# Keys of an attention kernel turned by DMA instead of TensorE, with the written order of work remade

## The chip, the cores and the metric

The kernel runs on one core of a Trainium2 chip. The metric is the time of one execution on the device in microseconds (us). The kernel before the change takes 297.64 us (median of three runs, 297.6 to 297.93). A core has five engines that run side by side and meet through semaphores: TensorE (PE, matmuls; PEld is its weight loading), VectorE (DVE), ScalarE (ACT), GpSimd (POOL) and SyncE (SP, which here only issues transfers). Transfers run on 16 DMA engines that all issuers share.

## The reference

Inputs are q, k, v of shape (4, 8, 768, 64) and two MLP weights, 512 x 2048 and 2048 x 512, all float32. For each batch and head the keys are averaged over 12 blocks of 64; each query takes the three blocks with the best gate score, and its own block:

```python
k_rep = k.reshape(B, H, n_blocks, block, D).mean(axis=3)
gate_scores = np.einsum('bhsd,bhnd->bhsn', q, k_rep)
gate_scores = np.where(causal, gate_scores, -1000000000.0)
top_idx = np.argsort(gate_scores, axis=-1)[..., -top_k:]
# mask: the chosen blocks and the own block, and causal
attn = softmax(where(mask, scale * q @ k.T, -1e9));  x = attn @ v
```

The heads are laid side by side (4, 768, 512) and go through a Fourier mixing layer:

```python
mixed = np.real(np.fft.fft(np.fft.fft(x, axis=1), axis=2))
u = x + mixed
un = (u - mean) / np.sqrt(var + 1e-06)
out = u + np.maximum(un @ w_ch1, 0.0) @ w_ch2
```

## The kernel before

**Tiling.** Work is cut into 16 head pairs P = 0 to 15, four for each of four batches. A pair's q and k come as float32 tiles of 128 positions x (6 position tiles, 2 heads, 64), a load of 192 KB for each head, and v in one load of 384 KB. For both q and k, PE transposes six 128x128 float32 tiles into PSUM (`a_tp`, L292; work items `tk` and `tq`). Of K's transposed tile DVE sums each 64 columns (`a_sums`, `ks`, L297), `a_half` (`kh`) splits these sums by head into the gate's weights, and ACT casts K to float16 into one of three slots `qk_s` (`a_k`, `kc`, L308 or L311). Of q's tile DVE makes a float32 copy (`a_q32`, `qc`, L316), which the gate uses, and GpSimd casts it into the slot (`a_q`, `qs`, through the helper `pcopy`, L225).

**Gate.** `g_mm` (`g`) multiplies q by the block sums in four strips of 32 columns, DVE turns the result (`gt`), takes the eight largest of each row (`gx`), compares (`gl`) and turns back (`gm`). For pairs 0 to 6 (`P < NX`) the mask is added to the scores by extra matmuls (L421). For pairs 7 to 15 it is copied by GpSimd into rows 64 to 95 of the slot (`stage_K`, item `K`), and one matmul of 96 rows makes score and mask together (L414); the key side of those 32 rows holds constant block indicators, loaded once a slot (L719, L733).

**Attention.** Scores of a pair come in six tiles (`s`), ACT takes exp (`e`, L431), GpSimd clears the part above the diagonal (`d`, L437), PE multiplies by v cast to float16 (`vc` on GpSimd, `v` on PE), and DVE divides (`x`). DVE folds the batch's x (`fs`, `fd`, `f`), PE does the two Fourier steps (`y`, L519; `m`, L552), DVE adds x (`u`), ACT centres (`xu`), and the result is transposed (`xt` on PE for batch 0; `un` by DMA, L593, for the others). The MLP is `w` (L629, L631), ReLU `r`, `c` (L656) and `o`, and SP stores (`od`).

**Order.** Nothing is scheduled by the program itself: the string `ORDER` lists all work items by hand, and each engine executes its own instructions in that order, waiting where an operand is missing. SP's transfers stand in one queue in that order too, and so do GpSimd's instructions, the weight loads that it issues included (`W` for three parts of w1, `X` for two halves of w2). PSUM has four tiles of two banks for everything. The first MLP matmul closes a first stretch in which the first batch's attention (and part of the second's) runs alone.

Of the kernel before, what the change touches and what calls it, by code (L numbers as in the profile page):

```python
# [11 lines left out]
FP = mybir.dt.float32  # L12
F16 = mybir.dt.float16
# [15 lines left out]
def _consts_np():  # L29
# [35 lines left out]
    ind = np.zeros((2, 32, S), np.float32)  # L65
    for e in range(2):
        ind[e, 16 * e:16 * e + NB] = nn[:, None] == (s[None, :] // 64)
# [5 lines left out]
                ind=ind.transpose(1, 0, 2).copy().astype(np.float16))  # L73
# [39 lines left out]
Lk:1 Lq:1 Lk:2 Lq:2 tk:0 ks:0 tq:0 Lq:3 Lk:3 kh:0 qc:0 iz:1 tk:1 qs:0 kc:0 g:0 ks:1 iz:0 gt:0 tq:1  # L113
kc:1 gx:0 Lq:4 Lv:0 Lk:4 Lv:1 kh:1 gl:0,0 tk:2 gl:0,1 gm:0 kc:2 qc:1 s:0,3 s:0,2 ks:2 e:0,3 qs:1
tq:2 Lq:5 Lk:5 s:0,5 qc:2 g:1 e:0,5 e:0,2 kh:2 s:0,4 gt:1 qs:2 s:0,0 e:0,4 gx:1 s:0,1 d:0,2 tq:3
gl:1,0 e:0,0 gl:1,1 tk:3 gm:1 e:0,1 d:0,0 qc:3 g:2 d:0,3 kc:3 d:0,5 s:1,5 gt:2 d:0,4 s:1,0 e:1,5
qs:3 ks:3 s:1,4 e:1,0 tq:4 d:0,1 gx:2 vc:0 e:1,4 s:1,3 qc:4 s:1,1 Lv:2 e:1,3 s:1,2 gl:2,0 kh:3
tk:4 gl:2,1 e:1,2 d:1,3 gm:2 g:3 d:1,4 ks:4 d:1,0 v:0 d:1,5 gt:3 vc:1 kc:4 gx:3 e:1,1 s:2,5 Lv:3
Lq:6 LF:0 Lq:7 Lk:6 Lk:7 LT:0 s:2,3 kh:4 gl:3,0 e:2,5 gl:3,1 s:2,4 e:2,3 d:1,1 x:0 tq:5 qs:4 e:2,4
g:4 d:2,3 gm:3 qc:5 s:2,0 d:2,4 s:2,2 d:1,2 e:2,0 gt:4 d:2,5 tk:5 vc:2 gx:4 e:2,2 s:2,1 ks:5 d:2,0  # L120
Lv:4 Lq:8 Lk:8 s:3,1 e:2,1 v:1 gl:4,0 kh:5 gl:4,1 kc:5 d:2,1 gm:4 d:2,2 s:3,2 x:1 e:3,1 vc:3 g:5
e:3,2 Lv:5 Lc:0 d:3,1 s:3,5 gt:5 s:3,0 fs:0,1 e:3,5 s:3,3 d:3,2 gx:5 e:3,0 s:3,4 fs:1,1 tq:6
gl:5,0 e:3,3 fs:0,0 v:2 gl:5,1 fs:1,0 e:3,4 d:3,3 qc:6 d:3,0 s:4,5 x:2 d:3,4 s:4,4 e:4,5 d:3,5
s:4,0 qs:5 v:3 e:4,0 gm:5 fs:2,0 fs:2,1 e:4,4 s:5,5 x:3 s:4,1 e:5,5 s:5,1 e:4,1 fd:2,0 s:4,2 s:5,0
fs:3,1 e:5,1 fs:3,0 s:5,2 fd:2,1 e:5,0 fd:3,1 s:4,3 fd:3,0 e:5,2 tk:6 f:0,1 f:0,2 e:4,3 Lk:9 Lq:9
tk:7 f:0,3 e:4,2 f:0,0 y:0,1 ks:7 pg:0 W:0 kc:6 y:0,0 tr:0,1 d:4,0 kc:7 d:4,4 d:4,5 ks:6 d:5,5
d:4,1 ty:0,1 tr:0,0 s:5,3 d:5,2 s:5,4 d:4,3 kh:6 W:1 ty:0,0 m:0,2 qs:6 e:5,3 u:0,2 m:0,1 vc:4
e:5,4 m:0,0 u:0,1 xu:0,2 d:5,4 tk:8 d:5,1 d:4,2 u:0,0 xu:0,1 d:5,0 xt:0,2 W:2 g:6 un:0,2 xu:0,0
xt:0,1 gt:6 tq:8 un:0,1 kc:8 xt:0,0 qc:8 tq:7 un:0,0 qs:8 v:4 Lq:10 Lk:10 Lv:6 Lq:11 qc:7 bn:0,3
w:0,4 d:5,3 qs:7 bn:0,1 w:0,5 r:0,4 gx:6 ks:8 w:0,6 r:0,5 gl:6,0 kh:7 gl:6,1 x:4 w:0,7 r:0,6 gm:6  # L130
w:0,3 r:0,7 s:6,5 r:0,3 s:6,1 e:6,5 s:6,3 e:6,1 kh:8 s:6,2 fs:4,0 bn:0,4 w:0,2 e:6,2 d:6,1 X:0
e:6,3 g:7 w:0,0 d:6,5 gt:7 r:0,2 d:6,3 vc:6 gx:7 s:6,4 r:0,0 vc:5 s:6,0 e:6,4 tk:9 Li:0 gl:7,0
Lv:7 tq:9 gl:7,1 e:6,0 gm:7 w:0,11 Lq:12 Lv:8 K:7 qc:9 kc:9 g:8 r:0,11 v:5 gt:8 d:6,0 ks:9 w:0,8
qs:9 gx:8 w:0,10 x:5 r:0,8 d:6,4 d:6,2 gl:8,0 s:7,5 s:7,2 r:0,10 kh:9 fs:4,1 w:0,1 bn:0,5 e:7,5
vc:7 e:7,2 tq:10 gl:8,1 Lv:9 r:0,1 X:1 gm:8 s:7,4 qc:10 w:0,15 d:7,2 e:7,4 K:8 bn:0,0 g:9 r:0,15
s:7,0 w:0,9 gt:9 e:7,0 gx:9 vc:8 tq:11 r:0,9 d:7,0 Lv:10 s:7,1 qc:11 d:7,5 tk:10 d:7,4 e:7,1
# [651 lines left out]
```

## Time and profile before

| what | value |
|---|---|
| median of the runs | 297.64 us |
| span of the profiled execution (its own time) | 295.6 us; the rest, 2.0 us, lies outside the span |
| PE transposes of q and k (L292) | 192, busy 27.5 us |
| DVE sums of K (L297) | 16 x 945 ns |
| ACT casts of K (L308 / L311) | 7 x 821 ns / 18 x 792 ns |
| GpSimd selections (L437) / cast copies of q | 96 x 414 ns / 25 x 825 ns |
| DMA transposes of `un` (L593) | 18 of 128x512, landing 2.5 us after issue |
| loads of k and q (192 KB) / v (384 KB) | landing 3.5 and 3.9 / 4.7 us after issue |
| weight loads on GpSimd's queue, 768 KB / 1 MB | landing 8.4 / 10.2 us after issue |

How to read it: a group's mean is the latency of one instruction; matmuls overlap, so a run of them passes faster than their means say. A row of 40 digits is the span in slices of 7.4 us, each digit the busy share in tenths. In a line of the timeline the first two numbers are start and duration, and what stands in brackets is idle time before it and what ended it.

### The profile page before, as it was taken

Reading aid. Unit: us, or ns where it says so; the run is one execution under the profiler, and the core shown is the slowest. Engines: PE = TensorE matmul, PEld = TensorE weight load, DVE = VectorE, ACT = ScalarE, POOL = GpSimd, SP = SyncE. Lnnn points to the kernel's source line nnn. Section 1 sums busy time; section 2 is a strip of 40 time slices with the busy share of each in tenths; the row PEclk is TensorE's granted clock in tenths of the full one; section 3 lists DMA queues with packets and bytes.
Section 4 is the critical chain, followed back from the end, with each engine's and each line's share of the span. In section 5 each row is a group of like instructions: output and inputs, shape, how many; then the busy total and the mean of one; then the engine's idle time right before and its main releaser. Section 6 shows DMA issues by size and latency. Waiting matters only on the chain.

```text
span 295.6 us, 6738 instructions
## 1 busy us (share of the span) xinstructions
PE 286.5 (97%) x2633; PEld 180.2 (61%) x2633; DVE 192.5 (65%) x597; ACT 164.2 (56%) x205; POOL 111.1 (38%) x286
## 2 busy tenths in 40 slices
PE   8899999999999999999999999999999999999995
PEld 4566767765676556656757667446666554555453
DVE  2999999986988638987796577714493282700132
ACT  3698989749578841677788843165524250155000
POOL 2267528528776289064753363220303000110000
PEclk9999999999999999999999999999999999999999
DMA  8999999997999727477000005311000052300023
GB/s 197 268 228 230 262 245 199 195 230 118 226 185 211 168 55 186 118 164 176 3 0 2 0 9 136 38 72 71 2 1 2 32 103 44 142 0 2 0 91 125
DMA packets 93200, 33.53 MB, mean 113 GB/s; under 512 B 85936, under 2 KB 89968, under 8 KB 93168
## 3 DMA queue, kind: packets, MB, share of 16 engines
q1 hardware_dynamic: 87504, 28.47, 40.6%
q0 software_dynamic: 3664, 4.19, 9.1%
q10 hardware_dynamic: 2000, 0.44, 0.7%
q8 instruction: 21, 0.34, 0.5%
q14 instruction: 11, 0.09, 0.1%
HBM read 28.63 MB, written 6.29 MB: 118 GB/s over the span
## 4 chain that ended last, share of the span: by engine, by line
PE 84%; DVE 7%; ACT 6%; DMA 1%; issue 1%; DVEq 0%; ACTq 0%
PE c L656 26%; PE h L629 19%; PE h L631 10%; PE sc L414 7%; PE av L449 6%; ACT pt L431 5%; PE tp L292 5%; PE yp L519 2%; PE mx L552 2%; DVE q L316 2%; PE mx L553 1%; PE warmps L693 1%; DVE u L566 1%; PE g L342 1%; PE c L648 1%; PE sc L409 1%
## 5 line engine op out<-in xcount | busy, mean ns | idle before, releaser
L431 ACT ACTIVATE pt<-sc 128x1024 f16<-128x1024 f32 (+1 forms) x96 | 83.3, 923 | 26.6 <-PE sc L414 19.7
L629 PE MATMUL h<-unT,w 128*128 128x512 f16 x256 | 85.1, 379 | 0.0
L656 PE MATMUL c<-w_sb,hT 128*128 128x512 f16 x368 | 83.8, 379 | 0.0
L631 PE MATMUL h<-unT,w 128*128 128x256 f16 x256 | 69.7, 272 | 0.4 <-DMA unT<-x 0.4
L641 ACT ACTIVATE hT<-h 128x768 f16<-128x768 f32 x48 | 37.8, 813 | 43.7 <-PE h L631 43.7
L656 PEld LDWEIGHTS <-hT 128*128 128x128 f16 x368 | 35.6, 98 | 39.3 <-issue 0.5
L437 POOL TENSOR_SCALAR_AFFINE_SELECT pt<-pt 128x256 f16<-128x256 f16 x96 | 37.5, 414 | 58.5 <-ACT pt L431 57.6
L629 PEld LDWEIGHTS <-w 128*128 128x128 f16 x256 | 25.0, 97 | 29.2 <-issue 1.3
L668 DVE SCALAR_TENSOR_TENSOR u<-c,rs,u 128x512 f32<-128x512 f32 (+1 forms) x25 | 17.5, 725 | 31.2 <-PE c L656 30.4
L639 DVE TENSOR_SCALAR hT<-h 128x768 f16<-128x768 f32 x16 | 15.3, 955 | 29.7 <-PE h L631 29.6
L578 ACT ACTIVATE x<-u,nm 128x512 f16<-128x512 f32 x24 | 15.9, 715 | 22.5 <-DVE nm L572 22.3
L292 PE MATMUL tp<-id,nat 128*128 128x128 f32 x192 | 27.5, 284 | 0.6 <-ACT pt L431 0.3
L631 PEld LDWEIGHTS <-w 128*128 128x128 f16 x256 | 25.0, 98 | 4.3
L225 POOL TENSOR_SCALAR_AFFINE_SELECT qk<-mt 32x160 f16<-32x160 f16 x72 | 23.1, 341 | 10.8 <-DVE mt L386 9.1
L414 PE MATMUL sc<-qk 96*128 96x512 f16 (+3 forms) x144 | 26.8, 305 | 0.0
L225 POOL TENSOR_SCALAR_AFFINE_SELECT qk<-q 64x768 f16<-64x768 f32 (+1 forms) x25 | 20.6, 825 | 14.8 <-DVE q L316 14.1
L292 PEld LDWEIGHTS tp<-id,nat 128*128 128x128 f32 x192 | 22.2, 146 | 5.7 <-issue 1.6
L449 PE MATMUL av<-v,pt 128*128 128x65 f16 x672 | 23.0, 193 | 0.1
L449 PEld LDWEIGHTS <-pt 128*128 128x128 f16 x672 | 22.0, 97 | 1.7 <-POOL pt L437 0.5
L297 DVE TENSOR_REDUCE kr<-tp 128x12 f32<-128x768 f32 x16 | 15.1, 945 | 5.9 <-PE tp L292 5.9
L222 POOL TENSOR_TENSOR t<-vr,rs 128x6 f32<-128x6 f32 x12 | 2.4, 199 | 43.5 <-DVE rs L609 42.9
L414 PEld LDWEIGHTS <-qk 96*128 96x128 f16 x144 | 13.3, 97 | 8.9 <-issue 0.5
(95 smaller groups left out, 351.2 us busy)
## 6 DMA issues: line engine op xcount, KB each, us to landing
nat<-in_v_dram SPq DMA_DIRECT2D x16, 384.0 KB, 4.7
nat<-in_k_dram SPq DMA_DIRECT2D x31, 192.0 KB, 3.5
nat<-in_q_dram SPq DMA_DIRECT2D x31, 192.0 KB, 3.9
out_dram<-u SPq DMA_DIRECT2D x23, 256.0 KB, 2.1
w_sb<-in_moe_w_ch_dram POOLq DMA_DIRECT2D x2, 1024.0 KB, 10.2
w<-in_moe_w_ch_dram POOLq DMA_DIRECT2D x2, 768.0 KB, 8.4
fs_sb<-c_FS SPq DMA_DIRECT2D x1, 582.0 KB, 5.1
w<-in_moe_w_ch_dram POOLq DMA_DIRECT2D x1, 512.0 KB, 7.3
```

What stands on the lines that cost most here:

```text
L225: nc.gpsimd.affine_select(out=out, in_=in_, pattern=[[0, i] for i in n], base=0, channel_multiplier=0, compare_op=ALU.is_ge, fill=0.0)
L292: nc.tensor.transpose(ps[:, 128 * st:128 * st + 128], src[:, st, :], id32)
L414: nc.tensor.matmul(ps[:, e, co:co + q1 - q0], qk[0:96, e, 1, 128 * jt:128 * jt + 128], qk[0:96, e, 0, q0:q1], start=True, stop=True)
L431: nc.scalar.activation(out=d["pt"][:, o:o + 2 * n].rearrange("p (e c) -> p e c", e=2), in_=d["sc", i][:, :, 0:n], func=AF.Exp, scale=0.125)
L437: nc.gpsimd.affine_select(out=dg, in_=dg, pattern=[[0, 2], [1, 128]], base=0, channel_multiplier=-1, compare_op=ALU.is_ge, fill=0.0)
L449: nc.tensor.matmul(av[:, e, 66 * st:66 * st + 65], pt[:, co:co + 128], vv[:, e, jt, 0:65], start=(cnt == 0), stop=(cnt == 20))
L578: nc.scalar.activation(out=x_b[:, 2 * kp + k2, :], in_=u_b[:, k2, :], func=AF.Identity, scale=0.0625, bias=nm[:, k2:k2 + 1])
L629: nc.tensor.matmul(hp[:, 0:512], w1s, unT[:, dt, 0:512], start=(dt == 0), stop=(dt == NDT - 1))
L631: nc.tensor.matmul(hp[:, 512:768], w1s, unT[:, dt, 512:768], start=(dt == 0), stop=(dt == NDT - 1))
L641: nc.scalar.activation(out=hT, in_=hp, func=AF.Relu)
L656: nc.tensor.matmul(c_ps[b, g[0]][:, st - g[0], :], h_t[b, it][:, 128 * st:128 * (st + 1)], w2_sb[:, it, :], start=(it == 0), stop=(it == N ...
L668: nc.vector.scalar_tensor_tensor(out=o, in0=ps, scalar=st_t[b][1][:, st:st + 1], in1=o, op0=ALU.mult, op1=ALU.add)
```

## The change

Pairs 0 and 1 keep the transposes on PE. For pairs 2 to 6, GpSimd casts K as loaded to float16 (`k_cast`, item `kn`) and SP issues one DMA transpose of 128x768 into the slot (`k_turn`, `kt`). For pairs 7 to 15, GpSimd issues a load that casts K to float16 in flight (`k_load`, `La`), beside constant indicators that already stand in the same tile (loaded once, `consts_next`), and SP issues two DMA transposes, one a head, which bring K and indicators to the slot together. The block sums of pairs 2 to 6 come from six small float32 matmuls on the natural K with the two columns of `half` (`k_blocks`, now under `tk`). For pairs 7 to 15, SP loads K a second time in rows of eight positions (96 partitions), GpSimd adds these by three halvings (`k_add`, `ka`), and one matmul with the constant `row8` sums them by blocks. Sums land in the gate's own PSUM tile, and `a_half` reads them there. The layout of a slot in pairs 7 on is q before k instead of head before head.

`ORDER` is written anew: the same work with the new items, in another order on every engine. At the front, GpSimd's queue is now `W:2`, `qs:0`, `X:1`, `qs:1`, `d:0,2`, `kn:2`, `W:1`; before, no weight was asked for until `pg:0` after the first fold. SP's queue begins `Lk:1 Lq:2 Lq:1 Lk:2 Lk:3 Lq:3 Lq:4 Lv:0 Lv:1 kt:2 Lq:5 Lk:5 LF:0 Lk:4 Lv:2 Lv:3 Lk:6 Lq:6 kt:3`.

```diff
 ORDER = """
-Lk:1 Lq:1 Lk:2 Lq:2 tk:0 ks:0 tq:0 Lq:3 Lk:3 kh:0 qc:0 iz:1 tk:1 qs:0 kc:0 g:0 ks:1 iz:0 gt:0 tq:1
-kc:1 gx:0 Lq:4 Lv:0 Lk:4 Lv:1 kh:1 gl:0,0 tk:2 gl:0,1 gm:0 kc:2 qc:1 s:0,3 s:0,2 ks:2 e:0,3 qs:1
+Lk:1 Lq:2 Lq:1 tk:0 iz:1 kc:0 tq:0 tk:1 kc:1 iz:0 ks:0 kh:0 qc:0 g:0 ks:1 tq:2 tq:1 gt:0 Lk:2 Lk:3
+Lq:3 Lq:4 Lv:0 W:2 qs:0 X:1 gx:0 gl:0,0 kh:1 gl:0,1 gm:0 s:0,0 s:0,2 e:0,0 e:0,2 qc:1 g:1 s:0,5
+s:0,3 e:0,5 s:0,1 s:0,4 tk:2 e:0,3 qc:2 gt:1 e:0,1 e:0,4 qs:1 d:0,2 kn:2 W:1 d:0,5 d:0,3 qs:2 vc:0
+kn:3 d:0,4 d:0,1 d:0,0 gx:1 gl:1,0 gl:1,1 gm:1 kh:2 tq:3 qc:3 g:2 s:1,5 e:1,5 s:1,1 s:1,4 s:1,3 gt:2
+tq:4 qc:4 tk:3 Lv:1 kt:2 Lq:5 Lk:5 LF:0 Lk:4 Lv:2 Lv:3 Lk:6 Lq:6 kt:3 e:1,1 e:1,3 e:1,4 s:1,0 kh:3
...
+    def nat1(P):
+        if P % 3 == 0:
+            t = ksrc[:, 0:S]
+        else:
+            t = k16n[P % 3 - 1].rearrange("p e st d -> p (e st d)").bitcast(FP)
+        return t.rearrange("p (st e d) -> p st e d", e=2, d=64)
...
+        if who == 1 and P >= NX:
+            eng.dma_start(ksrc[0:96].rearrange("p (e r) -> p e r", e=2),
+                          src[b, 2 * hp:2 * hp + 2].rearrange("e (p r) d -> p e (r d)", r=8))
+            return
...
+    def k_load(P):
+        b, hp = divmod(P, NP)
+        nc.gpsimd.dma_start(out=k16n[P % 2].rearrange("p e st d -> p (e st) d")[:, :, 0:64],
+                            in_=k[b, 2 * hp:2 * hp + 2].rearrange("e (st p) d -> p (e st) d", p=128))
+
+    def k_add(P):
+        x = ksrc[0:96].rearrange("p (e r) -> p e r", e=2)
+        tt(x[:, :, 0:256], x[:, :, 0:256], x[:, :, 256:512], ALU.add, nc.gpsimd)
+        tt(x[:, :, 0:128], x[:, :, 0:128], x[:, :, 128:256], ALU.add, nc.gpsimd)
+        pairs[P]["k8"] = k8 = spool.tile([96, 128], FP, tag="k8", name=f"k8_{P}", bufs=2)
+        tt(k8.rearrange("p (e d) -> p e d", e=2), x[:, :, 0:64], x[:, :, 64:128], ALU.add, nc.gpsimd)
+
+    def k_cast(P):
+        k16[P] = t = bpool.tile([128, S], F16, tag=f"hT{1 + P % 3}", name=f"k16_{P}")
+        pcopy(t, nat[P, 1].rearrange("p st e d -> p (st e d)"), [S])
+
+    def k_turn(P):
+        if P < NX:
+            nc.sync.dma_start_transpose(qk_s[P % NSLOT][:, 1, XW(P), :]
+                                        .rearrange("p (st c) -> p st c", c=128), k16[P])
+            return
+        for e in range(2):
+            nc.sync.dma_start_transpose(qk_s[P % NSLOT][:, 1, e, :]
+                                        .rearrange("p (st c) -> p st c", c=128),
+                                        k16n[P % 2][:, e].rearrange("p st d -> p (st d)"))
+
+    def k_blocks(P):
+        d = pairs[P]
+        d["slot"] = P % NSLOT
+        if P < NX:
+            d["g"] = g = pst([128, 300], f"g_{P}")
+            src = nat[P, 1].rearrange("p st e d -> p st (e d)")
+            for st in range(NST):
+                nc.tensor.matmul(g[:, 288 + 2 * st:290 + 2 * st], src[:, st, :], half[:, :, 0],
+                                 start=True, stop=True)
+            return
+        d["g"] = g = pst([128, 172], f"g_{P}")
+        nc.tensor.matmul(g[:, 160:172], d["k8"], row8, start=True, stop=True)
...
     def a_k(P):
         ps, qk = pairs[P]["tp", 1], qk_s[P % NSLOT]
-        if P < NX:
-            nc.scalar.copy(out=qk[:, 1, XW(P), :], in_=ps)
-        else:
-            for e in range(2):
-                nc.scalar.copy(out=qk[0:64, e, 1, :], in_=ps[64 * e:64 * e + 64])
+        nc.scalar.copy(out=qk[:, 1, XW(P), :], in_=ps)
...
-        for i in range(1, NSLOT):
-            nc.sync.dma_start(qk_s[i][64:96, :, 1, :], dr["ind"].ap())
+        nc.sync.dma_start(row8, dr["row8"].ap())
+        for t in k16n:
+            nc.sync.dma_start(t[:, :, :, 64:128].rearrange("p e st d -> p (e st) d"),
+                              dr["ind"].ap().rearrange("p (x d) -> p x d", d=64))
...
-        "tk": lambda P: a_tp(P, 1), "tq": lambda P: a_tp(P, 0), "ks": a_sums, "kh": a_half,
+        "tk": lambda P: k_blocks(P) if P >= KD[0] else a_tp(P, 1), "kn": k_cast, "kt": k_turn, "La": k_load, "ka": k_add, "tq": lambda P: a_tp(P, 0), "ks": a_sums, "kh": a_half,
```

## The prediction

> **What bounds the kernel now.** I read the page first, then the busy time in the two stretches before and after the first MLP matmul, then the DMA view in short windows, then the timeline around the first weight load.
>
> From the page:
>
> ```profile
> span 295.6 us, 6738 instructions
> PE 286.5 (97%) x2633; PEld 180.2 (61%) x2633; DVE 192.5 (65%) x597; ACT 164.2 (56%) x205; POOL 111.1 (38%) x286
> ...
> DVE  2999999986988638987796577714493282700132
> ...
> DMA  8999999997999727477000005311000052300023
> ...
> w<-in_moe_w_ch_dram POOLq DMA_DIRECT2D x2, 768.0 KB, 8.4
> ```
>
> Busy time by stretch (PE, PEld, DVE, ACT, POOL, clock, DMA share, GB/s):
>
> ```profile
> 0.00:58.60 58.60, 53.30 (x749) 38.24 (x750) 50.77 (x170) 47.18 (x59) 28.65 (x70) 1.00 1.05 228
> 58.60:292.20 233.60, 233.16 (x1890) 141.93 (x1886) 141.31 (x429) 117.06 (x146) 82.40 (x217) 1.00 0.37 84
> ```
>
> From 58.6 on PE never rests, so a microsecond of PE work there is a microsecond of time, and a later start of that stretch is added whole. Before it PE waits in small pieces, DVE is nearly full (50.8 of 58.6), and the DMA engines are full too. They are full yet nobody waits for them: no wait of PE in that stretch names a load. So loads run ahead of their use there, and the lead is what the change spends.
>
> DMA queues (packets, MB, share) from 2 to 12 us, from 53 to 59, and from 83 to 88; then SP in 84 to 91:
>
> ```profile
> DMA packets 10949, 2.68 MB, mean 268 GB/s; under 512 B 10949, under 2 KB 10949, under 8 KB 10949
> ```
>
> ```profile
> q0 software_dynamic: 771, 1.16, 112.0%
> q1 hardware_dynamic: 14, 0.00, 0.3%
> ```
>
> ```profile
> q0 software_dynamic: 811, 0.83, 110.3%
> q1 hardware_dynamic: 55, 0.01, 2.0%
> ```
>
> ```profile
> 84.97 4.81 SPq L270 DMA_DIRECT2D nat<-in_v_dram  x2
> ```
>
> q0 carries the weight loads that GpSimd issues, q1 everything of SP. With weights absent, 256-byte packets pass at 1095 per us, so a load of one pair's q, k or v (1536 packets) costs 1.4 us of DMA. With weights in flight q1 nearly stops: the V load issued at 84.97 lands 6.4 us later, when the weights are through. A 768 KB weight load (512 packets, 771 in 6 us) takes 4.0 us of DMA, a 1 MB one (1024, 811 in 5 us) 6.3 us.
>
> PE, and GpSimd's first weight load:
>
> ```profile
> 29.91 0.38 PE L409 MATMUL sc<-qk 64*128 64x256 f16 x4
> ...
> 44.97 1.78 PE L519 MATMUL yp<-fs_sb,fg 128*128 128x193 f16 x19
> ...
> 58.60 0.38 PE L629 MATMUL h<-unT,w 128*128 128x512 f16 x1
> ```
>
> ```profile
> 45.55 0.95 POOL L723 DMA_DIRECT2D w<-in_moe_w_ch_dram  x1
> ```
>
> Before, pair 3's scores begin at 29.9, the FFT matmuls at 45.0, the MLP at 58.6, and no weight is asked for until 45.5.
>
> **The change part by part.** The sum is made against the profiled execution: span 295.6, and about 2.0 us outside it, since the median of the runs is 297.64.
>
> *PE work.* Six transposes of a pair follow each other in 0.66 us (0.11 each). For pairs 7 to 15 they go, and one matmul of the block sums comes, which as float32 leaves two records (as the gate's matmuls do). Their nearest rows are the gate's, 8 records in 0.41 us (0.05 each), and the transposes' 0.11: 0.10 to 0.22 us a pair, I take 0.16. Seven of those pairs (9 to 15) were transposed after 58.6, so the full stretch loses 7 x 0.66 = 4.6 us and gains 9 x 0.16 = 1.4: net -3.2 (-2.6 to -3.7). For pairs 2 to 6, six transposes become six float32 matmuls with two columns, twelve records: 0.61 to 1.32 us against 0.66. The row of the float32 weight loads (median 140 ns for 128 columns, 106 for 32) makes the low end likelier; I book nothing, since PE has slack in that stretch. [...]
>
> *ACT and DVE.* Copies of K out of PSUM (0.8 us a pair on ACT, two of 0.8 for pairs from 7) and the sums over 64 keys (0.945 on DVE) go for 14 pairs. After 58.6 both engines had room: worth 0. Before 58.6 DVE loses the sums of pairs 2 to 8, 7 x 0.945 = 6.6 us of 50.8. With everything else in time this would be a gain of up to 6.6; from pair 3's scores on, about 2 of it (pairs 6 and 7) remain to be had.
>
> *Weights moved to the front.* This decides. GpSimd's queue now begins with the load of w1's last part (nothing waits before it, so issue near 2.4 us), then the cast of q for pair 0, the second half of w2, the cast of q for pair 1, one selection, the cast of K for pair 2, and w1's middle part. First packets come about 2.3 us after issue (47.9 for 45.55). So 4.0 us of weights enter the DMA engines near 4.7, 6.3 more some 10 us later and 4.0 right behind: 14.3 us of DMA in the first 27 us, each with the right of way that the windows show. Nothing needs them before the MLP.
>
> *The line of transfers.* On SP, K's transpose for pair 3 now stands behind 18 loads (k 0 to 6, q 0 to 6, v 0 to 3), the FD table and pair 2's transpose. From the first packet at 2.0: 18 x 1.4 = 25.2, FD 1.2 (landings 30.2 to 31.3), two transposes 1.4 (a 128x512 one makes 512 packets, so 768 at 1095 per us are 0.7 each), weights 14.3: 44.1, and about 1 us to land. Pair 3's scores cannot start before 45, where they began at 29.9. Without the weights the same line gives 31. On the way PE's queue holds pair 3's q transposes ahead of pair 1's scores: q 3 lands at 2.0 + 8 x 1.4 + 14.3 = 27.5, pair 1's scores, at 18.3 before, wait for it.
>
> *From pair 3 to the MLP.* Before: 58.6 - 29.9 = 28.7 us, through exp, selection, AV, fold, FFT and LayerNorm, mostly DVE and ACT. I keep it less the 2 us of sums: 45 + 26.7 = 71.7, that is +13.1. If ACT's freed time also counts, 25; if the transposes of pairs 4 and 5, two and six transfers later in the same line (about 48 and 53), are late too, 30: so +11 to +16. PE will idle some microseconds at a time there; the granted clock was 1.00 in all rows, and what idle time does to it no row shows, but matmuls do not set that stretch.
>
> *GpSimd, SP and DMA after 58.6.* Added on GpSimd for nine pairs: three adds over 512, 256 and 128 elements, and a cast load's issue. The rows that bound the adds are 0.2 us for 6 elements and 0.83 to 0.91 for one-input work on 768: 0.6 to 2.7 a pair (three of either), I take 1.6, the middle, since the sizes lie between; the issue is near the 0.83 of the weights'. 2.4 x 9 = 22 us on an engine busy 82 of 233.6. Five casts of 0.83 come earlier. SP issues 18 transposes of about 1.8 us (1.2 for four blocks, six here), 32 us, and stands still at each pair's first until the cast load lands; behind it wait later q, v and output transfers. The source of the adds has one buffer, so the next pair's load also waits on SP for GpSimd's adds. DMA was busy 37% in that stretch before, and the added transfers (per pair 192 packets of 2 KB and 1536 of the transposes, some 2.5 us, with 2 x 1536 packets of 128 bytes once) fit; so this is mostly covered; where a selection waits behind an add, PE's AV waits. I book +1 (0 to +5).
>
> Sum: 297.64 + 13.1 - 3.2 + 1 = 308.5.
>
> **The rivals.**
> 1. *The front weights are hidden and the lighter DVE sets the first stretch* (faster). For it: before, weights at 47 to 60 cost PE nothing, and DVE is at 87% up to 58.6. Against it: then the loads had a lead (k 5 landed at 24.8 and was transposed at 34.9), while in the first microseconds q 0 lands at 5.9 and is used at once. The stretch would end near 58.6 - 5, and PE's saving adds: 297.64 - 5 - 3.2 = 289.5 (288 to 293). It decides if weights take less than about 5 us from the line of loads before pair 3.
> 2. *Half of it:* the DMA loses only what the load of w1's last part takes, since w2's half comes after enough loads have landed, and the lighter DVE and ACT catch up: 297.64 + 8 - 3.2 - 1 = 301.5 (299 to 303). One point near no change, 297 to 298.2, lies between this and the first.
> 3. *GpSimd becomes a second bound.* Its 82 us after 58.6 become about 104, in order, with waits for landings inside; w1's first part and w2's first half are now asked for near 60, before the MLP, and can hold up q 7, whose transposes stand on PE ahead of the last LayerNorm transposes. The 6.3 + 3.2 us of those weights, or 5 us of late selections, come on top: 313 to 320.
>
> **How the numbers follow.** Main case 0.62 (303 to 313), rival 3 0.15, rival 2 0.08, rival 1 0.11, no change 0.04. A difference under 0.2% (0.6 us) is about what a measurement cannot tell. Slower 0.85, same 0.04, faster 0.11. Leaving out rival 1, no change and the top twentieth gives 298.5 to 319.
>
> **What would show it.** Right: q0 busy from about 5 us; PE idle in the first 30 us for a DMA of q; the share of PE under 8 tenths in several of slices 2 to 8; first MLP matmul near 72; after it PE full again for about 230 us; transposes x108 and 39 small float32 matmuls. Wrong: if the first MLP matmul comes before 60, the loads kept their lead and rival 1 holds; if it comes near 72 but the span exceeds 312, look for PE waiting for GpSimd or a K transpose after it.

## The result, and the profile after

| | before | after |
|---|---|---|
| median of four runs | 297.62 us | 349.88 us (345.97 to 351.69) |
| ratio after / before | | 1.172 (95% interval 1.164 to 1.179) |
| profiled execution: span | 295.6 us | 344.3 us |
| first MLP matmul | 58.6 us | 82.3 us (forecast 71.7) |
| from there to the last matmul | 233.5 us | 258.5 us (forecast 231.4) |

The change makes the kernel 52 us slower; 11 us had been forecast, and the range ended at 319. The direction was right, the size was not. The profiled execution is the fastest of the four; the ratio leaves out the slowest of them, which was in a slower state. In the profile the loss lies in both stretches: 23.7 us before the first MLP matmul and 25.0 behind it.

From the page of the kernel after (span, then busy time, then 40 slices of 8.6 us each):

```profile
span 344.3 us, 6768 instructions
...
PE 300.3 (87%) x2627; PEld 186.5 (54%) x2627; DVE 187.8 (55%) x583; ACT 147.0 (43%) x182; POOL 151.0 (44%) x327
...
PE   7665978699589997699959988999999999999995
...
PEclk9686696999989999899989999999999999999999
DMA  9999999999898799095399500005520004300043
```

PE was full from the eighth slice on before; now it has holes up to slice 25, and its clock, full throughout before, falls in eight of the first 21 slices. GpSimd works 151 us instead of 111.

The two stretches (PE, PEld, DVE, ACT, POOL, clock, DMA share, GB/s):

```profile
0.00:82.28 82.28, 63.47 (x767) 45.70 (x768) 48.62 (x162) 41.24 (x50) 38.92 (x79) 0.83 1.15 196
82.28:340.80 258.52, 236.87 (x1866) 140.76 (x1862) 138.67 (x421) 105.75 (x132) 112.09 (x249) 0.98 0.49 91
```

In the second stretch PE is idle for 21.6 us, where it had 0.4; in the first for 18.8 instead of 5.3. In the second it is also busy 3.7 us longer, though it has fewer matmuls, at a mean granted clock of 0.98. What ended PE's longest waits (total, times, longest):

```profile
PE sc L472 <- DMA qk<-k: 6.3, 3, 3.1
PE c L719 <- DVE u L731: 5.7, 2, 5.2
PE h L692 <- DMA unT<-x: 4.1, 1, 4.1
PE tp L313 <- DMA k16n<-in_k_dram: 4.0, 1, 4.0
PE tp L313 <- DMA nat<-in_q_dram: 3.8, 3, 2.0
PE g L350 <- DMA k16n<-in_k_dram: 2.6, 1, 2.6
PE g L354 <- POOL k L226: 2.6, 1, 2.6
PE sc L477 <- POOL qk L229: 2.2, 2, 1.4
```

No single wait is large. Loads, transposes by DMA, GpSimd and, through VectorE, GpSimd's Newton steps (the inverse square root of the LayerNorm) take turns. The rows that answer to those of the timeline before, GpSimd first, then PE:

```profile
2.36 0.96 POOL L788 DMA_DIRECT2D w<-in_moe_w_ch_dram  x1
...
52.80 0.29 PE L472 MATMUL sc<-qk 64*128 64x128 f16 x2 [3.13 <-DMA qk<-k]
...
69.06 1.13 PE L582 MATMUL yp<-fs_sb,fg 128*128 128x193 f16 x11 [1.73 <-DVE fg L564]
...
82.28 0.38 PE L692 MATMUL h<-unT,w 128*128 128x512 f16 x1
```

The first weights are asked for at 2.36, pair 3's scores begin at 52.8 (29.9 before, 45 forecast), the FFT at 69.1 (45.0), the MLP at 82.3 (58.6).

### The profile page after: what moved, and what is told of

It is laid out like the page before. It is cut to its first block, busy times and chain, and to the rows that moved or that the text cites. A ratio compares the mean times of both kernels' runs of the same rounds, so it can differ in the third digit from the quotient of the medians.

```text
span 344.3 us, 6768 instructions
## 1 busy us (share of the span) xinstructions
PE 300.3 (87%) x2627; PEld 186.5 (54%) x2627; DVE 187.8 (55%) x583; ACT 147.0 (43%) x182; POOL 151.0 (44%) x327
## 5 line engine op out<-in xcount | busy, mean ns | idle before, releaser
L692 PE MATMUL h<-unT,w 128*128 128x512 f16 x256 | 87.3, 387 | 5.3 <-DMA unT<-x 4.1
L719 PE MATMUL c<-w_sb,hT 128*128 128x512 f16 x368 | 85.5, 383 | 5.7 <-DVE u L731 5.7
L694 PE MATMUL h<-unT,w 128*128 128x256 f16 x256 | 71.1, 278 | 0.8 <-DMA unT<-x 0.8
L692 PEld LDWEIGHTS <-w 128*128 128x128 f16 x256 | 25.9, 101 | 33.3 <-DMA unT<-x 4.3
L226 POOL TENSOR_TENSOR t<-vr,rs 128x6 f32<-128x6 f32 x12 | 3.1, 257 | 69.7 <-DVE rs L672 69.0
L694 PEld LDWEIGHTS <-w 128*128 128x128 f16 x256 | 25.4, 99 | 6.2 <-DMA unT<-x 1.3
L229 POOL TENSOR_SCALAR_AFFINE_SELECT qk<-mt 32x160 f16<-32x160 f16 x72 | 24.7, 364 | 5.1 <-DVE mt L449 3.6
L512 PE MATMUL av<-v,pt 128*128 128x65 f16 x672 | 23.3, 193 | 1.1 <-POOL pt L500 0.8
L226 POOL TENSOR_TENSOR ksrc<-ksrc 96x512 f32<-96x512 f32 (+1 forms) x18 | 18.2, 1012 | 13.8 <-DMA ksrc<-in_k_dram 8.8
L512 PEld LDWEIGHTS <-pt 128*128 128x128 f16 x672 | 22.3, 97 | 3.1 <-POOL pt L500 1.2
L377 DVE COPY q<-tp 128x768 f32<-128x768 f32 x16 | 15.0, 945 | 13.6 <-PE tp L313 13.6
L472 PE MATMUL sc<-qk 64*128 64x512 f16 (+3 forms) x112 | 16.4, 343 | 6.7 <-DMA qk<-k 6.3
L629 DVE SCALAR_TENSOR_TENSOR u<-mx,x 128x512 f32<-128x512 f32 x24 | 15.6, 688 | 9.5 <-PE mx L616 9.5
```

Source lines behind the costliest of these rows:

```text
L226: (eng or nc.vector).tensor_tensor(out=out, in0=in0, in1=in1, op=op)
L229: nc.gpsimd.affine_select(out=out, in_=in_, pattern=[[0, i] for i in n], base=0, channel_multiplier=0, compare_op=ALU.is_ge, fill=0.0)
L472: nc.tensor.matmul(ps[:, e, co:co + q1 - q0], qk[hs[e], 1, XW(P), 128 * jt:128 * jt + 128], qk[hs[e], 0, XW(P), q0:q1], start=(co == 0), s ...
L512: nc.tensor.matmul(av[:, e, 66 * st:66 * st + 65], pt[:, co:co + 128], vv[:, e, jt, 0:65], start=(cnt == 0), stop=(cnt == 20))
L692: nc.tensor.matmul(hp[:, 0:512], w1s, unT[:, dt, 0:512], start=(dt == 0), stop=(dt == NDT - 1))
L694: nc.tensor.matmul(hp[:, 512:768], w1s, unT[:, dt, 512:768], start=(dt == 0), stop=(dt == NDT - 1))
```

## The experiments

"First MLP matmul" and "from there to the last" are read from each profile's timeline; they are called w and the second stretch. Ratios are to the kernel before, with 95% intervals.

### One part at a time

**Early weights alone, in the kernel before.** GpSimd's queue:

```diff
-qs:0 qs:1 qs:2 d:0,2 d:0,0 ...            (W:0 W:1 W:2 X:0 X:1 later)
+W:2 qs:0 X:1 qs:1 qs:2 d:0,2 W:1 d:0,0 ...
```

> The kernel before with nothing changed but three weight loads put to the front of GpSimd's queue, as in the changed kernel: the last part of w1 first, the second half of w2 behind the cast of q for pair 0, the middle part of w1 behind pair 0's first selection. If these 14.3 us of DMA take the lead of the loads by themselves: pair 3's scores about 10 us later than 29.9, the first MLP matmul at 66 to 73 instead of 58.6, 305 to 312 us. If the kernel before has lead enough (it loads keys and queries at 18 ns a packet and transposes on TensorE): the first MLP matmul within 3 us of 58.6, 296 to 301 us.

Ratio 1.039 (1.034 to 1.044), 309.8 us. The two stretches:

```profile
0.00:71.01 71.01, 56.23 (x749) 39.81 (x750) 51.74 (x170) 47.30 (x59) 29.28 (x71) 0.90 1.04 213
71.01:304.58 233.57, 233.15 (x1890) 142.00 (x1886) 141.11 (x428) 117.05 (x146) 81.34 (x216) 1.00 0.33 76
```

w comes at 71.0, 12.4 us later, and pair 3's scores at 42.0 instead of 29.9; the second stretch is what it was (233.57). The forecast had put 14.3 us of weights into the line of transfers, and this term holds in the main. That 71.0 is near the 71.7 of the forecast says less: that was for the whole change, not for the weights alone.

**Pairs 2 to 6 alone on the new path.** `kn:P kt:P` where `kc:P` was, the six matmuls of sums and `kh:P` shortly ahead of `g:P`, all in the order before:

```diff
-... tk:2 gl:0,1 gm:0 kc:2 ... ks:2 ... kh:2 ... g:2
+... gl:0,1 gm:0 kn:2 kt:2 ... tk:2 kh:2 ... g:2
```

> The new path of the keys for pairs 2 to 6 alone (cast on GpSimd, one transpose by DMA, six small matmuls of sums), in the order of work of the kernel before, weights where they were before. The early weights by themselves put the first MLP matmul at 71.0 instead of 58.6 us; the changed kernel has it at 82.3, so 11.3 us are left for this path and the order. If the path is the cause: the first MLP matmul at 66 to 72, then 233 us, 305 to 311 us. If the order is: within 3 us of 58.6, 296 to 301 us.

Ratio 1.033 (1.029 to 1.038), w at 68.9, second stretch 235.0. From its timeline (GpSimd, SP, PE):

```profile
31.90 0.86 POOL L224 TENSOR_SCALAR_AFFINE_SELECT k<-nat 128x768 f16<-128x768 f32 x1
...
45.34 1.33 SPq L301 DMA_TRANSPOSE qk<-k  x1
...
48.87 0.29 PE L431 MATMUL sc<-qk 64*128 64x128 f16 x2 [7.28 <-DMA qk<-k]
```

Pair 5's keys are cast at 32.8, but their transpose stands on SP behind loads of later pairs until 45.3, and PE waits 7.28 us. The reading is that the price is that of a place in a queue, not of a transpose. To test this, the same with pair 5's items ahead of `Lk:6 Lk:7`:

```diff
-... Lq:7 Lk:6 Lk:7 LT:0 ... kn:5 kt:5
+... Lq:7 kn:5 kt:5 Lk:6 Lk:7 LT:0 ...
```

> The run with pairs 2 to 6 alone on the new path, with one item moved: the cast and the transpose of pair 5's keys now stand ahead of the loads of keys 6 and 7 on their queues; before, the cast was done at 32.8 us, the transpose was asked for at 45.3, behind six loads, and TensorE waited 7.28 us for it at 48.9. If the place in SP's queue is the cost of these pairs (theory A): the wait goes, the first MLP matmul comes at 58 to 62, and 295 to 302 us; with the sums off VectorE it may come out below the kernel before. If transposes by DMA cost as such (theory B: slower line, late for the next pair too): another wait of 4 us or more takes its place, 304 to 309 us.

The wait is gone and the second stretch is back at 233.2, but w only moves to 65.4. The four runs took 303.7, 303.8, 308.3 and 314.2 us; the two fastest, one of them profiled, are 2% above the kernel before, and no interval is given. Neither theory came out: the wait went, as theory A had it, but w stayed later than its 58 to 62. So the place of pair 5's transpose cost 3.5 us of w, and 6.8 are left. In that profile no wait is longer than 1.7 us, the clock is half from 57.4 to 64.2 us, and six small matmuls (twelve records) stand in PE's way for each of five pairs:

```profile
54.74 1.40 PE L311 MATMUL g<-half,nat 128*128 128x2 f32 x12
```

**Pairs 7 to 15 alone**, in the order before, weights late:

```diff
-Lk:P ... tk:P ... ks:P ... kc:P ... kh:P ... g:P            (P = 7 to 15)
+ka:P kt:P Lk:P+1 La:P+1 (where ks:P was) ... tk:P kh:P ... g:P
```

> The new path of the keys for pairs 7 to 15 alone (cast load, adds on GpSimd, two transposes by DMA, one small matmul of sums), in the order of work of the kernel before; keys of pairs 0 to 6 go through TensorE, and the weights are asked for where they were before. If this path is what makes the stretch from the first MLP matmul on longer (258.5 us after, 233.6 before): the first MLP matmul near 58.6, then 248 us or more, 312 to 322 us. If the remade order does it (rival): 231 to 235 us from the first MLP matmul on, 294 to 300 us.

Ratio 1.096 (1.091 to 1.101), 326 us, above the 312 to 322 that had been expected: the largest part by far. w at 60.7; then, and the waits of PE:

```profile
60.67:321.41 260.74, 237.15 (x1860) 141.13 (x1860) 139.69 (x419) 106.34 (x132) 115.49 (x254) 0.97 0.56 100
```

```profile
PE g L354 <- POOL k L226: 9.9, 2, 7.2
PE h L694 <- DMA unT<-x: 3.5, 1, 3.5
PE g L405 <- DVE krb L226: 2.6, 1, 2.6
PE h L692 <- DMA w<-in_moe_w_ch_dram: 2.1, 1, 2.1
...
PE sc L477 <- POOL qk L229: 2.0, 1, 2.0
```

The second stretch is 27 us longer with the other work in the old order too. So the remade order is not needed for it; whether another place for the new items would make it shorter, this run does not show.

The three runs add up: 3.94 + 3.34 + 9.59 = 16.9% against 17.2% for the whole change. That does not make the parts independent: below, the changed kernel with late weights is as slow as with early ones. The +2.1 of w in the last is about that of the shifted tiles that it shares with the changed kernel (below). By stretches: w +12.4, +10.3 and +2.1 = 24.8 (23.7 measured), behind it 0 + 1.4 + 27.2 = 28.6 (25.0).

### What in pairs 7 to 15 costs 27 us

Each run leaves one part of that kernel out for the later pairs: `La:9` to `La:15`; `kt:10` to `kt:15`; `Lk:9` to `Lk:15` with `ka:9` to `ka:15`; and all of these.

> The run with pairs 7 to 15 alone on the new path, without the cast loads of pairs 9 to 15: the tiles keep the keys of pairs 7 and 8, so the scores of pairs 9 to 15 are those of other keys; transposes, adds and all else stay. A cast load is 1536 packets of 128 bytes at 32 ns, 3.1 us of all DMA engines, and 1.05 us of GpSimd; SP waits for it. If the cast loads are what fills the line (theory A): the waits after 90 us halve, 305 to 314 us of 326. If the transposes or the adds do it (rivals): 320 us or more.

> The same run with the cast loads and without the transposes by DMA of pairs 10 to 15: the scores of these pairs are those of the keys of pairs 7 to 9. Two transposes are 1536 packets, 2.0 us of DMA where nothing else runs, 2.6 us of SP's time for issuing, and SP stands before them until the cast load has landed and the slot is free. If transposes and the stand of SP's queue are the cost (theory A): 305 to 314 us of 326. If it is cast loads or the adds (rivals): 318 us or more.

> The run with pairs 7 to 15 alone on the new path, without the second load of the keys and the three adds for pairs 9 to 15: their block sums are those of pair 8, so other blocks are chosen; cast loads and transposes stay. The adds are 2.5 us of GpSimd a pair, the load is 192 packets, 1.4 us of DMA, into one buffer that SP waits for. TensorE's longest waits in that run were for the adds (7.22 and 2.73 us). If adds and their load hold the stretch from the first MLP matmul on (theory A): 260.7 us goes to 245 or less, 305 to 311 us. If it is the sum of all three parts on full queues, none of them alone (theory B): 250 to 256 us, 315 to 321 us, like the 252.3 without the cast loads.

> The same run without all three for the later pairs: no cast loads, second loads and adds from pair 9, no transposes by DMA from pair 10 (their scores and sums are those of earlier pairs); the order of what is left, the small matmul of sums and the shifted load tiles stay. If the three parts hold the stretch, separately or together: 231 to 237 us from the first MLP matmul on, 294 to 301 us. If the order, which I remade around these pairs, costs by itself: 245 us or more there, 308 us or more.

| left out | ratio (interval) | second stretch |
|---|---|---|
| nothing | 1.096 (1.091 to 1.101) | 260.7 |
| transposes | 1.084 (1.075 to 1.094) | 260.4 |
| second loads and adds | 1.076 (1.074 to 1.079) | 254.0 |
| cast loads | 1.069 (1.064 to 1.073) | 252.3 |
| all three | 1.048 (1.042 to 1.054) | 244.5 |

No part holds the stretch alone. The first time (318 us) falls between its two branches, the third came out as its theory B; without the transposes the time is within the noise of the kernel with everything. The last fits neither of its branches: its 244.5 us lie outside 231 to 237 and just under the 245 of the order, its 312.3 us in the order's range of 308 or more. Most of the 11 us that are left is one wait, which leads back over GpSimd to SP, and that is a matter of the place on the queues, of what was left in (pairs 7 and 8, and pair 9's transposes). From the timeline of the run without the three:

```profile
86.16 6.62 SPq L337 DMA_TRANSPOSE qk<-k16n  x2
...
102.03 1.98 POOL L227 TENSOR_SCALAR_AFFINE_SELECT v<-nat 128x768 f16<-128x768 f32 x1 [6.88 <-DMA nat<-in_v_dram]
...
107.33 1.86 PE L475 MATMUL sc<-qk 96*128 96x512 f16 x6 [8.96 <-POOL qk L227]
```

SP spends 86.2 to 92.8 on pair 9's two transposes; the load of v behind them lands at 102.0; GpSimd stands 6.88 us before that cast with the choice for pair 9 behind it; PE waits 8.96 us for the choice. SP's stand is only a part of why v is late: GpSimd had asked for 1 MB of weights at 88.0, and while these pass, few packets of SP's queue do (DMA from 92 to 98 us: packets, MB, share):

```profile
q0 software_dynamic: 931, 0.95, 103.8%
q1 hardware_dynamic: 420, 0.10, 16.4%
```

This chain is read from one trace. The run that should have shown SP's part takes the transposes off SP, and puts them somewhat later in the order:

```diff
-            nc.sync.dma_start_transpose(qk_s[P % NSLOT][:, 1, e, :]
+            nc.scalar.dma_start_transpose(qk_s[P % NSLOT][:, 1, e, :]
```

> The run with pairs 7 to 15 alone on the new path, with the transposes by DMA asked for by ScalarE instead of SP, and somewhat later in the order (where the sums were spread over the two heads). On SP they stood waiting for a cast load or a slot, up to 8.7 us, with loads of v and q behind them; with later cast loads, adds and transposes all left out, one wait of 8.96 us was left, which leads over the choice of pair 9 and a cast of v on GpSimd to loads of v behind pair 9's transposes. If SP's stand is the main cost of the path (theory A): loads of v no more late, 245 us or less from the first MLP matmul on, 305 to 312 us of 326. If the full line of transfers and GpSimd are (theory B), or ScalarE now stands in SP's place: 320 us or more.

Ratio 1.130 (1.124 to 1.136), second stretch 271.9: worse. PE now waits for ScalarE (9.1 us in one wait before scores, 5.4 in another), and ScalarE and SP wait for the keys (total, times, longest):

```profile
ACT hT L704 <- DMA qk<-k16n: 12.4, 1, 12.4
ACT pt L494 <- DMA qk<-k16n: 8.6, 1, 8.6
```

```profile
SPq L656 <- DMA qk<-k16n: 10.9, 2, 6.0
```

ReLU and exp now stand behind the transposes, and SP's own transposes of rows wait for a transfer that ScalarE asked for. So this run does not tell SP's stand apart from the rest; how the 27 us divide among the three parts stays open, beyond the table.

In the changed kernel itself, two attempts at relief. The Newton steps ahead of the keys' work, and rows' transposes ahead of a store and a load:

```diff
-... d:7,0 La:10 K:9 La:11 d:7,3 ka:11 nr:0 ...        un:1,0 od:0,4 Lk:14 un:1,1
+... d:7,0 nr:0 La:10 K:9 La:11 d:7,3 ka:11 ...        un:1,0 un:1,1 od:0,4 Lk:14
```

> The changed kernel with two items moved on their queues: on GpSimd the Newton steps of batch 0 go ahead of the two cast loads and the adds of pairs 10 and 11; on SP the transposes of batch 1's rows that stood behind an output store and pair 14's load go ahead of both. The changed kernel's TensorE waits 5.24 us at 140.5 for the first (through VectorE's last step of batch 0 and a PSUM buffer) and 4.12 us at 177.0 for the second. If these two queues hold the second stretch (theory A): both waits go and 338 to 343 us. If something else is late next behind them (theory B: keys of the later pairs, which then come later themselves): the waits only move, 347 to 352 us.

Ratio 1.199 (1.190 to 1.208), 357 us: slower than the change itself, beyond both theories. The wait for the rows is gone, but GpSimd now stands for VectorE, and PE waits 7.70 us for a selection queued behind (GpSimd's timeline):

```profile
128.49 0.20 POOL L226 TENSOR_TENSOR t<-vr,rs 128x6 f32<-128x6 f32 x1 [3.41 <-DVE rs L672]
```

The adds on VectorE:

```diff
-        tt(x[:, :, 0:256], x[:, :, 0:256], x[:, :, 256:512], ALU.add, nc.gpsimd)
+        tt(x[:, :, 0:256], x[:, :, 0:256], x[:, :, 256:512], ALU.add)
```

> The changed kernel with the three adds of each of the pairs 7 to 15 on VectorE in place of GpSimd, at the same place of the order. They take GpSimd 2.5 us a pair, and it is 88 to 93% busy from 100 to 140 us, where TensorE waits for selections, casts and Newton steps that stand behind them. If GpSimd's adds hold that stretch: GpSimd at 75% or less there, the 5.24 us wait at 140.5 gone or under 2 us, 335 to 342 us. If the line of transfers (cast loads, transposes) holds it: the waits stay, now put down to DMA, and 346 us or more.

Ratio 1.168 (1.164 to 1.173), no gain, though GpSimd's busy time falls from 151 to 130 us, and its share from 100 to 140 us from 90 to 67%: the wait at 140 shrinks to 2.67 us, that for the rows grows from 4.1 to 6.5. The second stretch gets only 1.2 us shorter (257.3), and w comes 4.8 later (87.1).

### Weights, clock and addresses in the first stretch

**The changed kernel with late weights:**

```diff
-W:2 qs:0 X:1 qs:1 d:0,2 kn:2 W:1 ... kn:6 La:7 ... W:0 d:4,0 X:0 ... ka:8 La:9 ... ka:9
+qs:0 qs:1 d:0,2 kn:2 ... kn:6 W:1 La:7 ... W:0 d:4,0 W:2 ... ka:8 X:0 La:9 ... ka:9 X:1
```

> The changed kernel with GpSimd asking for the weights late again: the middle part of w1 behind the cast of K for pair 6, its last part where the first half of w2 stood, the two halves of w2 behind the adds of pairs 8 and 9; all else, the line of transfers on SP too, as in the changed kernel. If the weights at the front are what makes the first stretch long (my prediction's step: 14.3 us of DMA in the line): first MLP matmul near 82.3 - 14 = 68, TensorE clock near 1 in the first 30 us, and 333 to 338 us. If the line itself, the casts and the transposes make it long (rival): first MLP matmul at 78 or later, 343 us or more.

w comes 9.8 us earlier, at 72.4: less than the 14 of the expectation, between its two branches. Pair 3's scores come at 40.9 instead of 52.8. But the second stretch grows to 273.5, and the ratio is 1.172 (1.164 to 1.179), the same as with early weights. A row of GpSimd's waits and one of PE's show part of where it went:

```profile
POOL ksrc L225 <- DMA ksrc<-in_k_dram: 21.9, 4, 11.2
```

```profile
PE g L353 <- POOL k L225: 9.7, 2, 6.8
```

The adds now wait 21.9 us for their loads (8.8 in the changed kernel), which share the DMA engines with the weights (1 MB is asked for at 93.6, and the longest of these waits, 11.25 us, ends at 112.2), and PE waits 9.7 us for the sums (2.6). The granted clock behind w is also half for 27 us instead of 10. So in this kernel late weights cost in the second stretch what they save in the first: 15 us for 10.

**TensorE kept busy in its waits:** matmuls on zeros ahead of `tk:1`, `tk:2`, `tq:3`, `tq:4` and `s:3,5`:

```diff
+    def warm(n):
+        wps = pst([128, 512], "warmps")
+        for _ in range(n):
+            nc.tensor.matmul(wps, wsrc[:, 0:128], wsrc, start=True, stop=True)
```

> The changed kernel with TensorE kept busy in five of its waits for DMA in the first stretch, by matmuls on zeros (20, 14, 9, 10 and 16 of 512 columns, about as long as the waits of 4.04, 2.59, 1.59, 1.99 and 3.13 us that they stand before). After those waits the granted clock was one half for four times 6.8 us, and TensorE was busy 63.5 us up to the first MLP matmul where it was 53.3 before. If the halved clock costs (theory A): no half clock there, the first MLP matmul 4 to 10 us earlier than 82.3, 338 to 346 us. If the loads set this stretch and the clock hides behind them (theory B): clock at one, first MLP matmul within 3 us of 82.3, 347 to 353 us.

From 6.7 to 37.4 us the granted clock is 1.00; the changed kernel ran 17 us of that at one half. (Later, 14 us before w are still at half.) w comes at 85.2 and the ratio is 1.167 (1.161 to 1.173): no gain, as theory B had it. The reading is that loads set that part and a slow PE hides behind them; the added matmuls may have cost some of what the clock gave, since w is 2.9 us later.

**Addresses.** The new tiles had moved every tile that a load writes by 64 bytes. (Addresses here are worked out from the sizes of the tiles in the order in which the kernel asks for them; no trace shows them.) Three kernels test that: the changed one moved back to multiples of 128, the one before with the shift alone, and a later one (below) moved back to the old addresses modulo 512.

```diff
+    pad = ctile([128, 16], FP, "pad")
     ksrc = ctile([128, 1024], FP, "ksrc")
```

> The changed kernel with one line more: 64 unused bytes ahead of the new tiles of the keys, so that every tile that a load writes starts at a multiple of 128 bytes, as in the kernel before (the new tiles had moved all load tiles by 64). Before, a 256-byte packet of a load took 18 ns in nearly every load; after, loads have means of 18 to 29 ns, up to 36 for one packet. If the address is the reason (theory A): 18 ns again, about 20 loads ahead of pair 3's scores each shorter by some 0.3 to 0.45 us, so pair 3's scores 5 to 9 us earlier than the 52.8 us seen, and 341 to 345 us. If the packets are slow because of what runs beside them, weight loads and transposes (theory B): packets as after, first MLP matmul near 82, 347 to 352 us.

> The kernel before with 64 unused bytes ahead of the tiles of v, so that every tile that a load writes starts 64 bytes off a multiple of 128, as in the changed kernel. There, with the shift, loads had packets of 18 to 33 ns from 4 us on, and with the shift taken back (the run with aligned loads) still 21 to 28 in the first 17 us, then mostly 18. If the address makes the packets slow: means of 22 to 26 ns in this kernel too, and 298 to 303 us, since loads run ahead of their use. If it is something else of the changed kernel: 18 ns and 297 to 299 us.

The shift alone costs the kernel before 0.5% (ratio 1.0054, 1.0022 to 1.0087), w 61.0 instead of 58.6. DMA from 8 to 14 us (packets, MB, share), shifted:

```profile
q1 hardware_dynamic: 5167, 1.30, 131.5%
```

Unshifted, the same six us carry 6421 packets at a share of 118.8%. So a packet takes about 24 ns instead of 18. Moved to multiples of 128, the changed kernel had means of mostly 21 to 28 ns up to 17 us and mostly 18 later, pair 3's scores at 52.9 as before, and a ratio of 1.161 (1.153 to 1.169), not to be told from 1.172: theory A of that run, with a period of 128, does not hold.

### A version without the waits

The new path for pairs 12 to 15 alone (pairs 0 to 11 through PE as before), where DMA has room (a share of 0.14 from 140 to 210 us in the kernel before), first with its items where the old ones stood, then behind the work PE had waited for, then at the old addresses modulo 512:

```diff
-K:11 vc:13 d:10,5 vc:12 ka:14 ... ka:15 K:12 La:15 qs:13 K:13 vc:15 ...   kt:12 od:0,0 od:0,1 un:1,1 un:1,0
+d:9,2 ka:12 d:10,3 K:11 vc:13 d:10,5 vc:12 ka:13 La:13 ... K:12 qs:13 K:13 vc:15 ka:14 La:14 ...   un:1,2 kt:12
```

```diff
-    pad = ctile([128, 16], FP, "pad")
-    lim = ctile([128, 4, 4], FP, "lim")
+    lim = spool.tile([128, 4, 4], FP, tag="lim", name="lim", bufs=1)
```

> The kernel before with the new path for pairs 12 to 15 alone, where DMA is 0 to 39% busy (it was 71 to 114% up to 100 us): load tiles at multiples of 128 bytes, order and weights as before, adds and cast loads at least 8 us ahead of their use. TensorE loses 24 transposes (2.6 us) and gains four small matmuls (0.6 us). If the path costs only where the line of transfers and GpSimd are full: no new wait over 1 us, 294 to 297.5 us. If it costs wherever it stands (SP's queue, adds): 300 us or more.

> The run with pairs 12 to 15 alone on the new path, with its items on GpSimd and SP moved: each pair's adds and cast load behind the work of GpSimd that TensorE waited for (the choice for pairs 11 and 13, the selections of pair 10), pair 12's transpose behind the transposes of batch 1's rows. Its waits were 1.84, 1.37 and 1.55 us for GpSimd and 3.17 us for the rows, and 245.4 us from the first MLP matmul on. If the place on the in-order queues is the cost of the path where DMA is quiet: those waits go, 232 to 236 us there, 295 to 300 us. If GpSimd's added 3.5 us a pair delay something wherever they stand: 240 us or more, 305 us or more.

> The run with pairs 12 to 15 alone and its items behind the work TensorE waited for, with its load tiles moved to the addresses modulo 512 that they have in the kernel before (a constant of 64 bytes goes to another pool in place of the 64 unused bytes). With the tiles at 128 modulo 512, 256-byte packets still had means of 25 ns from 5 to 18 us, and the first MLP matmul came at 59.9 where it was 58.6. If the address modulo 512 makes the packets slow (theory A): 18 ns throughout, first MLP matmul within 0.4 us of 58.6, 296 to 298 us, a little below the kernel before, since TensorE works 1.3 us less from there on. If something else of the kernel does it (theory B): 25 ns again and 298 to 299 us.

| | ratio (interval) | w | second stretch |
|---|---|---|---|
| items where the old ones stood | 1.043 (1.037 to 1.048) | 60.6 | 245.4 |
| items behind the awaited work | 1.003 (1.000 to 1.006) | 59.9 | 233.6 |
| and old addresses modulo 512 | 0.996 (0.994 to 0.998) | 58.6 | 232.8 |

PE's two longest groups of waits in the first of these, and what is left of the kind in the second:

```profile
PE sc L488 <- POOL qk L233: 5.1, 5, 1.8
PE h L705 <- DMA unT<-x: 3.2, 1, 3.2
```

```profile
PE h L706 <- DMA unT<-x: 0.9, 1, 0.9
```

The first time, 310.7 us, lies where the path was to cost wherever it stands; the second run shows that it need not. The same instructions cost 4% or nothing, by their place on GpSimd's and SP's queues alone. That holds where DMA has room; whether pairs 7 to 11 have such places, no run here tried. The third, for DMA from 8 to 14 us and by stretches:

```profile
q1 hardware_dynamic: 6472, 1.62, 119.8%
```

```profile
0.00:58.63 58.63, 53.10 (x749) 38.02 (x750) 50.80 (x170) 47.19 (x59) 28.69 (x70) 1.00 1.04 223
58.63:291.45 232.82, 231.56 (x1874) 140.02 (x1870) 140.74 (x424) 110.66 (x138) 96.40 (x233) 1.00 0.47 97
```

Packets are back at the old rate, w is back at 58.6, and PE does 1.6 us less from there on (231.56 for 233.16). It is 0.4% faster than the kernel before: little, but its interval leaves out 1.

## Why the prediction was wrong

- *Weights at the front, 14.3 us of DMA:* right in the main. Alone they move pair 3's scores by 12.1 and w by 12.4, and cost 11.7 us; in the changed kernel they move pair 3's scores by 11.9 (40.9 to 52.8). That q 3, forecast to land at 27.5, landed at 27.2 is partly luck: the third weight load's packets ran from 25.7 to 32.6, mostly behind it.
- *The line of transfers, pair 3's scores at 45:* too early by 7.8 us, and by 9.9 without the weights (31 forecast, 40.9 with late weights). The sum took the full rate of 1095 packets per us, at which a packet takes 18 ns, and a line that never stops. Packets took up to 29 ns a load, and the queues stood. GpSimd sat 8.48 us before a cast of v, with pair 3's cast of K behind it; yet that cast was done by 36.6, and SP, behind its loads, asked for the transpose only at 49.0. The stretch from there to the MLP, 26.7 by forecast, was 29.5. Together that is the 10.6 us between 71.7 and 82.3. Pairs 2 to 6 alone, in the old order, cost about as much (w +10.3), and the forecast had booked them at next to nothing (31 for 29.9).
- *PE work, -3.2:* right in kind. Four pairs save 1.6 us in the last kernel, 0.4 a pair against 0.5. The small matmuls of pairs 2 to 6 were mis-sized: 1.40 us for twelve records at full clock, a little beyond the end of the range that the transposes' row set (1.32). The gate's row (0.61), which I leaned to and whose weights have 32 columns and not 128, was the wrong one.
- *GpSimd, SP and DMA after 58.6, +1 (0 to +5):* **this is the step that failed.** With the PE term it made the second stretch 2.2 us shorter; that stretch grew by 25.0 us in the changed kernel and by 27.2 with pairs 7 to 15 alone, so with the forecast's 3.2 taken off PE the term is about 28 and 30, not 1. Three errors lie in it. The added transfers were put at 2.5 us of DMA a pair, but the cast load's own 1536 packets were left out: at 32 ns they take 3.1 us, beside 2.0 for the transposes and 1.4 for the second load, 6.5 in all where the old load took 1.7 (packet times over 16 engines). The adds were taken at 1.6 us a pair, the middle of the range; they take about 2.5, near its end (the page's row below, two adds a pair, and 0.45 for the third). And the mean share of 37% was read as room, although from 70 to 90 us the DMA engines were at 111 to 113% before the change; with the new path alone they were at 124 to 141% from 70 to 110.

```profile
L226 POOL TENSOR_TENSOR ksrc<-ksrc 96x512 f32<-96x512 f32 (+1 forms) x18 | 18.2, 1012 | 13.8 <-DMA ksrc<-in_k_dram 8.8
```

- *Rival 3* (GpSimd a second bound, 313 to 320) named the right engine and rows, but took the waits as added to an order that otherwise kept time. GpSimd's busy time alone was not the bound: with 21 us less of it the second stretch got only 1.2 us shorter. In order, a late landing holds what stands behind it, on SP's, GpSimd's and PE's queues in turn, as in the chain of 6.88 us on GpSimd and 8.96 on PE above; how much each holds the runs do not tell apart.
- *Rivals 1 and 2* (hidden, or half hidden): the weights were not hidden.
- *The clock*, left without a price: it was halved for about 38 us in all (27 before w, 10 behind), but filling five waits of the first stretch, which brought its 27 us down to 14, gained nothing. In the second stretch nothing was filled, so what it cost there is open; by estimate PE's own work is at most 5 us of the 25 longer for it, since a 512- and a 256-column matmul of the MLP together start every 0.64 us at half clock (from 178.0 us) and every 0.33 at full clock (from 180.8), so 10 us at half clock hold about 5 us of work.
- *What would show it:* q0 busy early (from 6.6 us; 5 was forecast), waits for q in the first 30 us, PE below 8 tenths in several of slices 2 to 8, and the counts of transposes and small matmuls came true; the first MLP matmul near 72 and PE full behind it did not.

## What to carry to other kernels

Before work is moved to DMA and in-order queues, count every packet of it at the packet times of the profile, stage by stage, and not against the mean share of the span. For each instruction that can wait (a transpose on SP, an add or cast on GpSimd), name what stands behind it: here the same instructions cost 4% or nothing by their place, where DMA had room. When a tile is added ahead of load tiles, look at the addresses of all that follow: here a shift by 64 bytes took packets from 18 to 24 ns (8 to 14 us) and cost 0.5%.

## What the runs showed of the hardware that was not expected

**The granted clock went to one half, for 3.4 or 6.8 us at a time.** In the kernel after, PE idles 4.04 us up to 11.6 and 2.59 us up to 23.3; the stretches around (columns as above, the clock third from the end):

```profile
6.62:10.03 3.41, 0.88 (x6) 0.64 (x6) 1.03 (x3) 1.53 (x2) 0.00 (x0) 1.00 1.22 204
10.03:16.86 6.83, 5.09 (x25) 3.51 (x26) 3.88 (x18) 1.53 (x2) 1.69 (x2) 0.50 1.27 221
16.86:23.68 6.82, 4.07 (x63) 2.35 (x61) 4.49 (x17) 4.96 (x6) 1.58 (x3) 1.00 1.22 214
23.68:30.51 6.83, 5.24 (x37) 3.81 (x38) 1.62 (x3) 0.26 (x1) 2.75 (x5) 0.50 1.14 191
```

The stretches at 0.50 in this kernel's profile are four of 6.8 us before w and three of 3.4 behind it. The one from 10.0 us begins inside the wait of 4.04 us, the one from 23.7 follows the wait of 2.59, and the one from 33.9 one of 1.99. A wait of 1.73 us, up to 69.1, was followed by full clock, so what decides it these runs do not show.

**The address of a load's tile changed the packet time.** With the tiles of q and k at multiples of 512 bytes, packets from 8 to 14 us took 18 ns (the kernel before, and the last version); at 64 bytes beyond, in the kernel before with the shift alone, 24 ns; at 128 beyond, in the version ahead of the last, 25. Addresses do not explain all. At 128 beyond, that version moved 216 and 204 GB/s in the slices from 7.4 to 22.3 us, but 239, 250 and 262 in the three behind them, where the kernel before moved 268 and 228, then 230, 262 and 245. And tiles of v stood at 128 beyond a multiple of 512 in the kernel before: of two loads issued at 112.75 us, packets took 18 ns from 114.3 to 115.6 us and 24 from 115.8 to 117.1. So how the address sets the packet time is not settled by these runs.

**A cast load by GpSimd was dear for its size.** Its 1536 packets of 128 bytes at 32 ns took 3.1 us of all 16 DMA engines, almost twice the 1.7 us (1536 at 18 ns) of the float32 load of the same keys. One alone, in the kernel after from 121.9 to 123.9 us (packets, MB, share):

```profile
q0 software_dynamic: 1552, 0.20, 153.9%
```
